# Linear attention into a gated FFN: first load in fp32 on another queue, narrow z matmuls, a new order on VectorE in the prologue, a new PSUM ring order, last stores on two queues

## Chip, cores, metric

One core of a Trainium2 chip. The metric is device time in microseconds (us), median of several runs. Engines: PE is TensorE (matmul; PEld its weight loads), DVE is VectorE, ACT is ScalarE, POOL is GpSimd, SP is SyncE, which issues DMAs.

## The reference

```python
def phi(x): return np.where(x > 0, x, np.exp(x) - 1.0) + 1.0
# q, k, v: [8 batches, 8 heads, 576 tokens, 64]
q_p, k_p = phi(q), phi(k)
kv  = einsum('bhsd,bhse->bhde', k_p, v)
z   = sum(k_p, axis=2)
num = einsum('bhsd,bhde->bhse', q_p, kv)
den = einsum('bhsd,bhd->bhs', q_p, z)[..., None] + 1e-06
x   = (num / den)  -> [4608 tokens, 512]
g   = x @ w_gate                                   # 512 -> 1536
out = (g / (1 + exp(-g)) * (x @ w_val)) @ w_out    # 1536 -> 512
```

## The kernel before

The tokens go through the FFN in nine groups of 512. While PE works on the FFN of one group, DVE and ACT prepare the next one. Group 0 has nothing to hide behind: its preparation is the *prologue*. Batches 0 and 1 get special code: phi(q) is transposed on PE, the reciprocal of den is exp(-ln(den)) on ACT.

The prologue (names: `mx_k`, `mn_k`, `add_k` are the DVE steps of phi(k); `zt` sums phi(k) over tokens by matmuls with a block of ones; `Zr` is z spread over 64 columns; `t_corners` multiplies with qT; `lnrd` is ln and exp on ACT; `warm` issues matmuls on ones whose results nothing uses):

```python
    WARM = (20, 8, 10, 2, 4)
    def warm(n):                        # n matmuls of 128x256 on ones
    def zt(b, lp, ps, t, first, last):
        for j in range(J):              # J = 9
            nc.tensor.matmul(out=ps[:, 0:P], lhsT=t[b % 2][:, lp, j, :], rhs=ob[:, :], ...)   # P = 128
    def lnrd(ps, i, w0=0, w1=512):
        for l2 in range(2):
            act(osb[2 * i + l2][:, w0:w1], ps[l2][:, w0:w1], AF.Ln, bias=epsb[:, 0:1])
            act(rd[i][:, l2, w0:w1], osb[2 * i + l2][:, w0:w1], AF.Exp, scale=-1.0)
    ...
    ld(q, qr, 0, 0)                     # POOL's queue, fp32 -> fp16 on the way
    ld(q, qr, 0, 1)
    ld2(k, kr, 0)
    ...
    mx_k(0, 0);  ph[1][1]();  zt(0, 0, .., kp, ..);  warm(WARM[3])
    t_add_half(1, pq[1], 0);  mn_k(0, 0);  zt(0, 0, .., ek, ..)
    add_k(0, 0);  zr_copy(0, 0, ..);  warm(WARM[4])
    t_add_half(1, pq[1], 1);  t_corners(0, Zr, 0, pp4[2]);  lnrd(pp4[2], 0)
    kv_corner(0, 0, ..);  mx_k(0, 1);  r_copy(0, 0, 1, "VV");  mn_k(0, 1);  t_corners(0, R, 0, pp4[0])
    ...
```

The seam between group 0 and group 1. PE holds four pairs of PSUM banks in a ring. `osb` are the tiles from which outputs are stored; before the change `lnrd` used them for its logarithms too:

```python
        def s7():
            ...
            exp_k(2, 0);  exp_k(2, 1)
            lnrd(cq, 0, 0, 256)                         # writes and reads osb[0], osb[1] on ACT
        def s8():
            for t in range(4):
                l2_out(0, t, "V")                       # DVE: PSUM -> osb[t], then stored
            xmul(xT[0] ..., cq ..., rd ...)             # two: the last two token blocks of group 1
        ...
        exp_q(2, 0);  exp_q(2, 1);  phi_k(2, 0);  phi_k(2, 1)
        ring[:] = [dz, cq, l2p[(0, "p", 0)], l2p[(0, "p", 1)]]
```

"Period 1" below is the FFN of group 1 and what runs beside it.

Of the kernel before, what the change touches and what calls it, by code (L numbers as in the profile page):

```python
# [13 lines left out]
P = 128  # L14
# [3 lines left out]
def kernel(  # L18
# [16 lines left out]
    C = 64  # L35
# [4 lines left out]
    EPS = 1e-6  # L40
    SC = 4096.0
    NB = 3
    WARM = (20, 8, 10, 2, 4)

    sb = ctx.enter_context(tc.tile_pool(name="sb", bufs=1))
    pp = ctx.enter_context(tc.tile_pool(name="ps", bufs=1, space=bass.MemoryType.PSUM))
# [15 lines left out]
    Zr = many([P, 2, 2, D], FP16, "Zr")  # L62
    rd = many([P, 2, 512], FP16, "rd")

    prod = sb.tile([P, J, 2 * D], FP16, name="prod")
    den = sb.tile([P, 2, J * 2], FP32, name="den")
    rden = sb.tile([P, 2, J * 2], FP32, name="rden")
# [30 lines left out]
    def ld(src, dst, b, lp):  # L98
        nc.gpsimd.dma_start(out=dst[b % NB][:, 2 * lp:2 * lp + 2, :],  # L99
                            in_=src[b].rearrange("(l a) (c j) d -> (a c) l (j d)", a=2, j=J)[:, 2 * lp:2 * lp + 2, :])  # L100
# [14 lines left out]
    def act(out, in_, func=AF.Copy, scale=1.0, bias=0.0):  # L115
        nc.scalar.activation(out=out, in_=in_, func=func, bias=bias, scale=scale)  # L116

    def warm(n):
        for _ in range(n):
            nc.tensor.matmul(out=pp4[2][1][:, :].rearrange("p (a b) -> p a b", a=4)[:, 0:2, :],  # L120
                             lhsT=ones[:, :], rhs=ones[:, :].unsqueeze(1).to_broadcast([P, 2, P]), start=True, stop=True)

    def hs(lp):
        return slice(2 * lp, 2 * lp + 2)
# [28 lines left out]
    def add_k(b, lp):  # L153
        a = kp[b % 2][:, lp, :, :]
        nc.vector.tensor_tensor(out=a, in0=ek[b % 2][:, lp, :, :], in1=a, op=ALU.add)  # L155
# [19 lines left out]
    def kv_corner(b, lp, t, first, last):  # L175
        ps = kvp[b]
        for j in range(J):
            for l2 in range(2):
                for hh in range(2):
                    rows = slice(C * hh, C * hh + C)  # L180
                    nc.tensor.matmul(out=ps[hh][D * l2:D * l2 + D, D * lp:D * lp + D],  # L181
                                     lhsT=t[b % 2][rows, lp, j, D * l2:D * l2 + D],
                                     rhs=vr[b % NB][rows, 2 * lp + l2, D * j:D * j + D],
                                     start=(first and j == 0), stop=(last and j == J - 1))
# [6 lines left out]
    def r_copy(b, l0, l1, engs):  # L191
        for hh in range(2):
            src = kvp[b][hh][:, D * l0:D * l1].rearrange("p (l d) -> p l d", d=D)
            if engs[hh] == "A":
                act(R[b % 3][:, l0:l1, hh, :], src)
            else:
                nc.vector.tensor_copy(out=R[b % 3][:, l0:l1, hh, :], in_=src)
# [112 lines left out]
    def l2_out(g, t, eng, n0=0, n1=512, o=None):  # L310
        if o is None:
            o = osb[on[0] % 4]
            on[0] += 1
        ps = l2p[(g, t)]
        if eng == "A":
            act(o[:, n0:n1], ps[:, n0:n1], scale=1.0 / SC)
        else:
            nc.vector.tensor_scalar(out=o[:, n0:n1], in0=ps[:, n0:n1], scalar1=1.0 / SC, scalar2=None, op0=ALU.mult)  # L318
        for e in range(2):
            b, j = units(g)[0][2 * t + e]  # L320
            nc.sync.dma_start(out=out[S * b:S * b + S, n0:n1].rearrange("(c j) f -> j c f", j=J)[j],
                              in_=o[C * e:C * e + C, n0:n1])
        return o



    ld(q, qr, 0, 0)
    ld(q, qr, 0, 1)
    nc.gpsimd.iota(out=idx[:, :], pattern=[[-1, P]], base=0, channel_multiplier=1)
    ld2(k, kr, 0)  # L330
# [49 lines left out]
    def t_phi_main(b, lp, ps):  # L380
        return t_phi(qT[b][:, lp, 0:8, :, :].rearrange("p j h c -> p (j h c)"), ps[:, :].bitcast(FP16))
# [4 lines left out]

    def zt(b, lp, ps, t, first, last):
        for j in range(J):
            nc.tensor.matmul(out=ps[:, 0:P], lhsT=t[b % 2][:, lp, j, :], rhs=ob[:, :],  # L389
                             start=(first and j == 0), stop=(last and j == J - 1))  # L390

    def zr_copy(b, lp, ps):
        nc.vector.tensor_scalar(out=Zr[b][:, lp, :, :].rearrange("p h e -> p (h e)"), in0=ps[:, 0:P],
                                scalar1=1.0 / SC, scalar2=None, op0=ALU.mult)

    def lnrd(ps, i, w0=0, w1=512):
        for l2 in range(2):
            act(osb[2 * i + l2][:, w0:w1], ps[l2][:, w0:w1], AF.Ln, bias=epsb[:, 0:1])
            act(rd[i][:, l2, w0:w1], osb[2 * i + l2][:, w0:w1], AF.Exp, scale=-1.0)

    def xmul(dst, ps, r):
        nc.vector.scalar_tensor_tensor(out=dst, in0=ps, scalar=1.0 / SC, in1=r, op0=ALU.mult, op1=ALU.mult)  # L402
# [5 lines left out]
    def t_corners(g, W, lp, ps):  # L408
        for (b, j0, j1, c0) in units(g)[1]:
            corners(ps, W[b], b, lp, j0, j1, c0)  # L410

    def t_add_half(lp, ps, h):
        a = qT[0][:, lp, 4 * h:4 * h + 4, :, :].rearrange("p j h c -> p (j h c)")
        nc.vector.scalar_tensor_tensor(out=a, in0=ps[:, 256 * h:256 * h + 256].bitcast(FP16), scalar=0.0, in1=a,  # L414
                                       op0=ALU.max, op1=ALU.add)

    pq = pp4[0]
    kvp[0] = pp4[1]
    ph = [t_phi_main(0, lp, pq[lp]) for lp in range(2)]
    warm(WARM[0])  # L420
    for lp in range(2):
        qtr(0, lp, pq[lp])
# [4 lines left out]
    ph[0][1]()  # L427
    ph[0][2]()
    mx_k(0, 0)
    ph[1][1]()  # L430
    zt(0, 0, pp4[3][0], kp, True, False)
    warm(WARM[3])
    t_add_half(1, pq[1], 0)
    mn_k(0, 0)
    zt(0, 0, pp4[3][0], ek, False, True)
    add_k(0, 0)
    zr_copy(0, 0, pp4[3][0])
    warm(WARM[4])
    t_add_half(1, pq[1], 1)
    t_corners(0, Zr, 0, pp4[2])  # L440
    lnrd(pp4[2], 0)
    kv_corner(0, 0, kp, True, True)
    mx_k(0, 1)
    r_copy(0, 0, 1, "VV")
    mn_k(0, 1)
    t_corners(0, R, 0, pp4[0])
    zt(0, 1, pp4[3][1], kp, True, False)
    zt(0, 1, pp4[3][1], ek, False, True)
    x_t(0, 0, pp4[0], (0,))
    zr_copy(0, 1, pp4[3][1])  # L450
    t_corners(0, Zr, 1, pp4[3])
    lnrd(pp4[3], 1)
    kv_corner(0, 1, kp, True, False)
# [28 lines left out]
    def p1_z():  # L482
        b1p["z"] = kvp[1] = pair()
        ring.pop()
        for lp in range(2):
            ps = b1p["z"][0]
            nc.tensor.matmul(out=ps[:, P * lp:P * lp + P], lhsT=zs[:, lp, 0, :], rhs=ob[:, :], start=True, stop=True)
        nc.vector.tensor_scalar(out=Zr[1][:, :, :, :].rearrange("p l h e -> p (l h e)"), in0=ps[:, 0:2 * P],
                                scalar1=1.0 / SC, scalar2=None, op0=ALU.mult)

    def period0():
# [28 lines left out]
    def layer2_0():  # L520
        for t in range(4):
            l2_open(0, t)
        p1_z()
        p1_open()
        cq, dz = b1p["q"], b1p["z"]
        p8 = [t_phi_8(b, dz[0]) for b in range(2)]
        pm = [t_phi_main(1, lp, cq[lp]) for lp in range(2)]
        nc.scalar.preload_act_table_set("natural_log_exp_and_others")

        def den(lp, ps):  # L530
            t_corners(1, Zr, lp, ps)
            lnrd(ps, lp)

        def kvr(lp):
            kv_corner(1, lp, kp, True, True)
            r_copy(1, lp, lp + 1, "VV")

        def nx(lp, ps):
            t_corners(1, R, lp, ps)
            x_t(1, lp, ps)  # L540

        def s0():
            qtr(1, 0, cq[0])
            for f in pm[0]:
                f()

        def s1():
            qtr8(dz[0])
            for f in (0, 1, 2):
                for b in range(2):  # L550
                    p8[b][f]()

        def s2():
            den(0, dz)

        def s3():
            qtr(1, 1, cq[1])
            for f in pm[1]:
                f()

        def s4():
            den(1, cq)

        def s5():
            kvr(0)

        def s6():
            kvr(1)
            nx(0, cq)

        def s7():
            nx(1, dz)
            for lp in range(2):
                corners(cq, Zr[1], 1, lp, 7, 9, P * lp)
                corners(cq, R[1], 1, lp, 7, 9, 256 + P * lp)
            exp_k(2, 0)
            exp_k(2, 1)
            lnrd(cq, 0, 0, 256)

        def s8():  # L580
            for t in range(4):
                l2_out(0, t, "V")
            for l2 in range(2):
                xmul(xT[0][:, l2::2, 0:P], cq[l2][:, 256:512].rearrange("p (l c) -> p l c", l=2),
                     rd[0][:, l2, 0:256].rearrange("p (l c) -> p l c", l=2))

        step = {1: [s0], 3: [s1, s3], 6: [s2], 7: [s4], 9: [s5], 10: [s6], 11: [s7]}
        for fb in range(FB):
            if fb in step:
                for f in step[fb]:  # L590
                    f()
            for t in range(4):
                l2_mm(0, t, fb)
        s8()
        exp_q(2, 0)
        exp_q(2, 1)
        phi_k(2, 0)
        phi_k(2, 1)
        ring[:] = [dz, cq, l2p[(0, "p", 0)], l2p[(0, "p", 1)]]

    for g in range(NG):
        b1, b2 = g + 1, g + 2
# [95 lines left out]
```

## Time and profile before

| | us |
|---|---|
| median time (3 runs) | 320.79 (320.46 to 321.27) |
| span in the profile | 319.0 |
| steady FFN matmuls begin (end of the prologue) | 22.02 |
| period 2 begins | 89.67 |
| last ACT copy ends / span ends | 315.37 / 319.0 |

From the page of the profile, part 1, the busy time of each engine and its share of the span; PE is the limit:

```profile
PE 307.7 (96%) x2240; PEld 145.9 (46%) x2240; DVE 203.5 (64%) x354; ACT 150.9 (47%) x227; POOL 49.2 (15%) x74
```

The list of PE's waits (who waited for whom: total, times, longest):

```profile
PE pp L364 <- DMA qr<-in_q_dram: 1.8, 2, 1.2
PE pp L288 <- DVE xT L402: 1.4, 1, 1.4
...
PE pp L181 <- issue: 0.8, 1, 0.8
```

Outside the prologue there is one wait of weight, 1.4 us for DVE's xT. The timeline around it (start, length, engine, line, operation, result<-operands, and in brackets the idle time before with what ended it):

```profile
53.44 1.04 PE L295 MATMUL pp<-wo,hT 128*128 128x512 f16 x4
53.60 0.45 ACT L116 ACTIVATE osb<-pp,epsb 128x256 f32<-128x256 f32 x1
54.09 0.42 ACT L116 ACTIVATE rd<-osb 128x256 f16<-128x256 f32 x1
...
54.32 1.03 PE L288 MATMUL pp<-xT,wg 128*128 128x512 f16 x4
...
54.54 2.70 DVE L318 TENSOR_SCALAR osb<-pp 128x512 f32<-128x512 f32 x4 [0.24 <-ACT rd L116]
...
57.15 0.75 DVE L402 SCALAR_TENSOR_TENSOR xT<-pp,rd 128x256 f16<-128x256 f32 x2
...
57.63 0.39 PE L288 MATMUL pp<-xT,wg 128*128 128x512 f16 x1 [1.42 <-DVE xT L402]
```

The second pair that PE asks for is `cq`, which the two xT operations at 57.15 still read.

The windows view (busy time of PE, PEld, DVE, ACT and POOL in a stretch, then granted clock, DMA share and GB/s) for 54.5 to 86 us:

```profile
54.50:86.00 31.50, 30.08 (x228) 13.70 (x229) 30.60 (x56) 18.60 (x28) 2.21 (x4) 1.00 0.58 117
```

DVE is busy 30.60 of 31.50 us here. It is the limit in this stretch as much as PE is.

The chain of waits that ended last has two marks of time (start, length, what): the first long run of FFN matmuls of group 0, and that of group 2.

```profile
22.02 17.27 PE pp L288 x80
...
89.67 20.72 PE pp L288 x96
```

### The profile page before, as it was taken

The numbers are of one execution on the slowest core, as the hardware profiler recorded it, in microseconds if no ns is written. First come the engines' busy times: TensorE is split into PE (matmuls) and PEld (weight loads), VectorE is DVE, ScalarE is ACT, GpSimd is POOL, SyncE is SP. The second block draws the span as 40 slices with busy tenths as digits, with TensorE's granted clock in tenths as the row PEclk, the third lists the DMA queues.
The fourth block names the chain that finished last, engine by engine and source line by source line (L and its number), as shares of the span: only waits on it lengthen the run. The fifth ranks groups of instructions, "written<-read, shape, count | busy, mean of one in ns | idle before, by whom it ended". The sixth has DMA issues, their size and how long they took to land.

```text
span 319.0 us, 5630 instructions
## 1 busy us (share of the span) xinstructions
PE 307.7 (96%) x2240; PEld 145.9 (46%) x2240; DVE 203.5 (64%) x354; ACT 150.9 (47%) x227; POOL 49.2 (15%) x74
## 2 busy tenths in 40 slices
PE   6789999899999999999999999999999999999994
PEld 4544444344544454444444454445444444444443
DVE  2844865999849874987498749973992344133410
ACT  2764859646643474347534753385331333133211
POOL 8665343000400050006000500000000000000000
PEclk9999999999999999999999999999999999999999
DMA  7999999931693379038903790225023400140014
GB/s 96 196 198 198 206 206 206 249 69 37 99 232 67 73 96 249 13 74 118 234 7 71 107 239 14 47 41 123 0 39 70 99 1 3 33 99 2 0 35 97
DMA packets 41162, 32.21 MB, mean 101 GB/s; under 512 B 16432, under 2 KB 36656, under 8 KB 41136
## 3 DMA queue, kind: packets, MB, share of 16 engines
q0 software_dynamic: 21008, 18.88, 38.6%
q1 hardware_dynamic: 20128, 12.98, 16.9%
q8 instruction: 17, 0.28, 0.3%
q14 instruction: 9, 0.07, 0.1%
HBM read 37.75 MB, written 9.44 MB: 148 GB/s over the span
## 4 chain that ended last, share of the span: by engine, by line
PE 93%; DVE 3%; DMA 2%; issue 1%; POOL 1%; ACT 0%; POOLq 0%; DVEq 0%
PE pp L288 57%; PE pp L295 29%; DMA kr<-in_k_dram 2%; PE pp L250 2%; PE pp L181 2%; PE pp L272 1%; DVE osb L318 1%; POOL qr L99 0%; DVE qT L414 0%; PE pp L389 0%; DVE xT L402 0%; PE pp L364 0%; DVE kp L139 0%; DVE kp L155 0%; PE pp L208 0%
## 5 line engine op out<-in xcount | busy, mean ns | idle before, releaser
L116 ACT ACTIVATE sil<-pp 128x512 f16<-128x512 f32 x108 | 63.4, 597 | 103.3 <-PE pp L288 98.8
L288 PE MATMUL pp<-xT,wg 128*128 128x512 f16 x424 | 108.8, 379 | 1.4 <-DVE xT L402 1.4
L288 PE MATMUL pp<-xT,wv 128*128 128x512 f16 x424 | 108.8, 379 | 0.0
L281 DVE SCALAR_TENSOR_TENSOR hT<-pp,sil 128x512 f16<-128x512 f32 x108 | 72.1, 681 | 47.8 <-PE pp L288 34.6
L295 PE MATMUL pp<-wo,hT 128*128 128x512 f16 (+1 forms) x444 | 97.5, 374 | 0.5 <-DVE osb L318 0.5
L288 PEld LDWEIGHTS <-wg 128*128 128x128 f16 x424 | 41.4, 98 | 51.1 <-DVE xT L402 1.9
L295 PEld LDWEIGHTS <-hT 128*128 128x128 f16 x444 | 42.1, 98 | 48.7 <-issue 1.9
L288 PEld LDWEIGHTS <-wv 128*128 128x128 f16 x424 | 41.5, 98 | 50.0
L318 DVE TENSOR_SCALAR osb<-pp 128x512 f32<-128x512 f32 (+1 forms) x20 | 13.3, 675 | 31.6 <-PE pp L295 26.8
L116 ACT ACTIVATE osb<-pp 128x512 f32<-128x512 f32 (+1 forms) x17 | 9.8, 578 | 34.9 <-PE pp L295 34.9
L116 ACT ACT_TABLE_LOAD x14 | 18.0, 1283 | 2.8 <-PE pp L288 2.6
L116 ACT ACTIVATE ek<-kr 128x1152 f16<-128x1152 f16 x16 | 17.8, 1154 | 0.3 <-DMA kr<-in_k_dram 0.2
L633 POOL COPY gate<-qT 128x1 f16<-128x1 f16 x4 | 1.3, 336 | 106.7 <-DMA qT<-qp 57.4
L225 DVE TENSOR_TENSOR qp<-qp,rden 128x1152 f16<-128x1152 f16 x12 | 16.2, 1346 | 0.0
L216 DVE TENSOR_REDUCE den<-prod 128x18 f32<-128x1152 f16 x12 | 16.1, 1345 | 0.0
L267 DVE TENSOR_SCALAR xT<-pp 128x512 f16<-128x512 f32 (+1 forms) x14 | 8.8, 667 | 7.3 <-PE pp L250 7.3
L116 ACT ACTIVATE eq<-qr 128x1152 f16<-128x1152 f16 x12 | 13.2, 1147 | 0.0
L99 POOL DMA_DIRECT2D kr<-in_k_dram x16 | 11.6, 726 | 6.8 <-DMA wo<-in_moe_w_out_dram 1.9
L99 POOL DMA_DIRECT2D vr<-in_v_dram x16 | 11.8, 742 | 5.2 <-DMA wo<-in_moe_w_out_dram 1.9
L99 POOL DMA_DIRECT2D qr<-in_q_dram x16 | 11.6, 729 | 6.0 <-DMA wo<-in_moe_w_out_dram 1.8
L155 DVE TENSOR_TENSOR kp<-ek,kp 128x1152 f16<-128x1152 f16 x15 | 11.4, 759 | 0.6
L143 DVE TENSOR_SCALAR ek<-ek 128x1152 f16<-128x1152 f16 x16 | 7.4, 463 | 4.8 <-ACT ek L116 4.8
(66 smaller groups left out, 175.6 us busy)
## 6 DMA issues: line engine op xcount, KB each, us to landing
out_dram<-osb SPq DMA_DIRECT2D x70, 128.0 KB, 5.3
qr<-in_q_dram POOLq DMA_DIRECT2D x16, 288.0 KB, 11.7
kr<-in_k_dram POOLq DMA_DIRECT2D x16, 288.0 KB, 6.6
vr<-in_v_dram POOLq DMA_DIRECT2D x16, 288.0 KB, 9.5
wo<-in_moe_w_out_dram POOLq DMA_DIRECT2D x3, 512.0 KB, 13.0
wg<-in_moe_w_gate_dram POOLq DMA_DIRECT2D x5, 256.0 KB, 9.6
wv<-in_moe_w_val_dram POOLq DMA_DIRECT2D x5, 256.0 KB, 10.2
wg<-in_moe_w_gate_dram POOLq DMA_DIRECT2D x2, 128.0 KB, 8.3
```

Of the source, the lines that this page charges most:

```text
L99: nc.gpsimd.dma_start(out=dst[b % NB][:, 2 * lp:2 * lp + 2, :], in_=src[b].rearrange("(l a) (c j) d -> (a c) l (j d)", a=2, j=J)[:, 2 * lp ...
L116: nc.scalar.activation(out=out, in_=in_, func=func, bias=bias, scale=scale)
L143: nc.vector.tensor_scalar(out=a, in0=a, scalar1=1.0, scalar2=None, op0=ALU.min)
L155: nc.vector.tensor_tensor(out=a, in0=ek[b % 2][:, lp, :, :], in1=a, op=ALU.add)
L181: nc.tensor.matmul(out=ps[hh][D * l2:D * l2 + D, D * lp:D * lp + D], lhsT=t[b % 2][rows, lp, j, D * l2:D * l2 + D], rhs=vr[b % NB][rows, 2 ...
L216: nc.vector.tensor_reduce(out=den[:, c, :], in_=prod[:, :, :].rearrange("p j (l d) -> p (j l) d", d=D), axis=AX.X, op=ALU.add)
L225: nc.vector.tensor_tensor(out=qv, in0=qv, in1=rden[:, c, :].unsqueeze(2).to_broadcast([P, 2 * J, D]), op=ALU.mult)
L267: nc.vector.tensor_scalar(out=dst, in0=ps[l2][:, c0:], scalar1=1.0 / SC, scalar2=None, op0=ALU.mult)
L281: nc.vector.scalar_tensor_tensor(out=hT[g % 2][:, fb, :], in0=ps[1][:, :], scalar=SC, in1=s[:, :], op0=ALU.mult, op1=ALU.mult)
L288: nc.tensor.matmul(out=ps[h][:, :], lhsT=w[:, c, P * fb:P * fb + P], rhs=xT[g % 2][:, c, :], start=(c == 0), stop=(c == 3))
L295: nc.tensor.matmul(out=l2p[(g, t)][:, n0:n1], lhsT=hT[g % 2][:, fb, P * t:P * t + P], rhs=wo[:, fb, n0:n1], start=(fb == 0), stop=(fb == F ...
L318: nc.vector.tensor_scalar(out=o[:, n0:n1], in0=ps[:, n0:n1], scalar1=1.0 / SC, scalar2=None, op0=ALU.mult)
```

## The change

Its intent: start the prologue earlier, get to the first Zr sooner, remove the wait for xT at 57 us, and issue the last two stores side by side. The diff, cut:

```diff
-    WARM = (20, 8, 10, 2, 4)
+    WARM = (36, 10, 20, 8, 6)
+    q32 = sb.tile([P, 2, J * D], FP32, name="q32")
+    lnt = many([P, 512], FP32, "lnt", 4)
     def warm(n):   # 128x256 -> 128x128 per matmul
-    ld(q, qr, 0, 0)
+    nc.sync.dma_start(out=q32[:, :, :], in_=q[0] ... [:, 0:2, :])
+    for l in range(2):
+        nc.vector.tensor_copy(out=qr[0][:, l, :], in_=q32[:, l, :])
     def zt(b, lp, ps, t, first, last):
-            nc.tensor.matmul(out=ps[:, 0:P], lhsT=t[b % 2][:, lp, j, :], rhs=ob[:, :],
+            nc.tensor.matmul(out=ps[:, 0:2], lhsT=t[b % 2][:, lp, j, :], rhs=ob[:, 0:P:C],
     def lnrd(ps, i, w0=0, w1=512):
-            act(osb[2 * i + l2][:, w0:w1], ps[l2][:, w0:w1], AF.Ln, bias=epsb[:, 0:1])
+            act(lnt[2 * i + l2][:, w0:w1], ps[l2][:, w0:w1], AF.Ln, bias=epsb[:, 0:1])
     ...  # batch 0 on DVE: mn_k before the min step of q's second half; zr_copy, then mx_k and mn_k of k's
     ...  # second half, before add_k(0, 0); the half adds of qT after that; z of batch 1 by 2 columns too
-        ring[:] = [dz, cq, l2p[(0, "p", 0)], l2p[(0, "p", 1)]]
+        ring[:] = [dz, l2p[(0, "p", 0)], l2p[(0, "p", 1)], cq]
-            nc.sync.dma_start(out=out[...], in_=o[...])
+            dma = nc.scalar if g == NG - 1 and t == 3 and n1 == 512 and e == 1 else nc.sync
+            dma.dma_start(out=out[...], in_=o[...])
```

More of the change, by code (lines that the diff above doesn't have):

```diff
@@ L119, in warm @@
         for _ in range(n):
-            nc.tensor.matmul(out=pp4[2][1][:, :].rearrange("p (a b) -> p a b", a=4)[:, 0:2, :],
-                             lhsT=ones[:, :], rhs=ones[:, :].unsqueeze(1).to_broadcast([P, 2, P]), start=True, stop=True)
+            nc.tensor.matmul(out=pp4[2][1][:, 0:P], lhsT=ones[:, :], rhs=ones[:, :], start=True, stop=True)
     def hs(lp):
@@ L320, in l2_out @@
             b, j = units(g)[0][2 * t + e]
-            nc.sync.dma_start(out=out[S * b:S * b + S, n0:n1].rearrange("(c j) f -> j c f", j=J)[j],
+            dma = nc.scalar if g == NG - 1 and t == 3 and n1 == 512 and e == 1 else nc.sync
+            dma.dma_start(out=out[S * b:S * b + S, n0:n1].rearrange("(c j) f -> j c f", j=J)[j],
                               in_=o[C * e:C * e + C, n0:n1])
         return o
-    ld(q, qr, 0, 0)
+    nc.sync.dma_start(out=q32[:, :, :],
+                      in_=q[0].rearrange("(l a) (c j) d -> (a c) l (j d)", a=2, j=J)[:, 0:2, :])
     ld(q, qr, 0, 1)
@@ L388, in zt @@
         for j in range(J):
-            nc.tensor.matmul(out=ps[:, 0:P], lhsT=t[b % 2][:, lp, j, :], rhs=ob[:, :],
+            nc.tensor.matmul(out=ps[:, 0:2], lhsT=t[b % 2][:, lp, j, :], rhs=ob[:, 0:P:C],
                              start=(first and j == 0), stop=(last and j == J - 1))
     def zr_copy(b, lp, ps):
-        nc.vector.tensor_scalar(out=Zr[b][:, lp, :, :].rearrange("p h e -> p (h e)"), in0=ps[:, 0:P],
+        nc.vector.tensor_scalar(out=Zr[b][:, lp, :, :], in0=ps[:, 0:2].unsqueeze(2).to_broadcast([P, 2, D]),
                                 scalar1=1.0 / SC, scalar2=None, op0=ALU.mult)
@@ L397, in lnrd @@
         for l2 in range(2):
-            act(osb[2 * i + l2][:, w0:w1], ps[l2][:, w0:w1], AF.Ln, bias=epsb[:, 0:1])
-            act(rd[i][:, l2, w0:w1], osb[2 * i + l2][:, w0:w1], AF.Exp, scale=-1.0)
+            act(lnt[2 * i + l2][:, w0:w1], ps[l2][:, w0:w1], AF.Ln, bias=epsb[:, 0:1])
+            act(rd[i][:, l2, w0:w1], lnt[2 * i + l2][:, w0:w1], AF.Exp, scale=-1.0)
     def xmul(dst, ps, r):
@@ L429 @@
     mx_k(0, 0)
-    ph[1][1]()
     zt(0, 0, pp4[3][0], kp, True, False)
     warm(WARM[3])
-    t_add_half(1, pq[1], 0)
     mn_k(0, 0)
     zt(0, 0, pp4[3][0], ek, False, True)
-    add_k(0, 0)
+    ph[1][1]()
     zr_copy(0, 0, pp4[3][0])
     warm(WARM[4])
-    t_add_half(1, pq[1], 1)
     t_corners(0, Zr, 0, pp4[2])
     lnrd(pp4[2], 0)
-    kv_corner(0, 0, kp, True, True)
     mx_k(0, 1)
-    r_copy(0, 0, 1, "VV")
     mn_k(0, 1)
-    t_corners(0, R, 0, pp4[0])
     zt(0, 1, pp4[3][1], kp, True, False)
     zt(0, 1, pp4[3][1], ek, False, True)
+    add_k(0, 0)
+    kv_corner(0, 0, kp, True, True)
+    zr_copy(0, 1, pp4[3][1])
+    t_add_half(1, pq[1], 0)
+    r_copy(0, 0, 1, "VV")
+    t_add_half(1, pq[1], 1)
+    t_corners(0, R, 0, pp4[0])
     x_t(0, 0, pp4[0], (0,))
-    zr_copy(0, 1, pp4[3][1])
     t_corners(0, Zr, 1, pp4[3])
@@ L486, in p1_z @@
             ps = b1p["z"][0]
-            nc.tensor.matmul(out=ps[:, P * lp:P * lp + P], lhsT=zs[:, lp, 0, :], rhs=ob[:, :], start=True, stop=True)
-        nc.vector.tensor_scalar(out=Zr[1][:, :, :, :].rearrange("p l h e -> p (l h e)"), in0=ps[:, 0:2 * P],
+            nc.tensor.matmul(out=ps[:, 2 * lp:2 * lp + 2], lhsT=zs[:, lp, 0, :], rhs=ob[:, 0:P:C],
+                             start=True, stop=True)
+        nc.vector.tensor_scalar(out=Zr[1][:, :, :, :].rearrange("p l h e -> p (l h) e"),
+                                in0=ps[:, 0:4].unsqueeze(2).to_broadcast([P, 4, D]),
                                 scalar1=1.0 / SC, scalar2=None, op0=ALU.mult)
```

## The prediction

> **What bounds the kernel.** TensorE: the busy table gives PE 96% of the 319.0 us span, and the chain that ended last is 93% PE (the two FFN matmul lines 57% and 29%). From 17.9 us PE hardly pauses, so a gain can come from three places only.
>
> 1. *Prologue.* The steady FFN matmuls begin at 22.0 us (timeline). The chain there: k's first half lands at 9.6, DVE work to 13.9, then Zr and R corners, ACT logarithms until 19.0, xT at 20.7. q's halves are first used at 5.3 and 8.1. From 3.5 us the DMA engines are full (190 GB/s written), with a dip to 95 GB/s from 6 to 8.
> 2. *The gap before period 1.* The list of PE's waits has 1.4 us, at 56.2 to 57.6, for DVE's xT: the second pair in the ring is the one DVE still reads.
> 3. *Tail.* The last ACT copy ends at 315.37; SP issues two stores one after the other (0.47 and 0.59 us), the second at 315.92, landing 2.0 later.
>
> **What the change does.**
>
> - *q in fp32 by SP's queue.* The bytes read from HBM stay. It frees one POOL issue of 0.78 us, so k, v and weights are issued that much earlier. [...]I expect no more bandwidth, only an earlier start. The price: two DVE casts, estimated at 0.4 to 0.6 us each from the 128x1152 fp16 operations (0.46 us; 0.58 beside POOL issues). First transposes at 5.5 to 6 us, second at 7, k at 8.7.
> - *DVE order, narrow z.* The first Zr comes before add_k (0.76 us) and a half add of qT (0.69), so the Zr corners start at about 11.5 instead of 12.7. [...]Prologue in all: 1.3 us (0.3 to 2.0).
> - *Ring order.* The 1.4 us wait goes. But the windows show DVE busy 30.6 of 31.5 us from 54.5 to 86.0, without a wait on PE over 0.25: the last hT of period 1 is ready at 78.96 by DVE's own work, and its matmul starts at 79.3 already. The second numerator pair at 85.7 needs DVE's copy that ends at 85.72. So nearly all of the 1.4 comes back as a wait of PE's layer-2 matmuls for hT near 78. Net 0.1 us (0 to 0.3).
> - *Last stores on two queues.* The second issue no longer follows the first: 0.5 us.
> - *Warm-up matmuls, separate lnt tiles:* nothing.
>
> **Sum.** 1.3 + 0.1 + 0.5 = 1.9 us: 318.9 us, 8 times in 10 within 317.6 to 320.1. Faster by over 2% (below 314.4) 2%, within 2% 97%, slower 1%.
>
> **What would show it.** PE's waits: none for xT at 56 us, but a new one of 1.2 to 1.5 us of the layer-2 line on DVE hT in period 1. Timeline: steady FFN matmuls from about 20.7 us; k at 8.5 to 9; Zr corners near 11.5. The span ends 0.5 us sooner after the last copy.
>
> **What would make it wrong.** The fp32 load shares engines with q's second quarter and lands after 6.5 us; [...]weights too late for the earlier start; a stall like the unexplained 0.8 us "issue" gap of PE at 16.9; or DVE slack in period 1 that I missed (then 1.3 us more).

To check two figures against the trace of before: from 3.5 to 6 us the core moved 191 GB/s at a DMA share of 1.18, and from 6.5 to 7.5 us, the dip, 94 to 97 GB/s. The "0.58 beside POOL issues" are the two DVE operations at 13.18 and 13.94 us, while POOL issued loads at 12.76, 13.49 and 14.22; what made them longer is not shown.

## The result

The changed kernel takes 319.39 us (318.84 to 319.74, 4 runs), before takes 320.62 us (320.26 to 321.27, 4 runs) in the same series: 1.2 us less. The ratio is 0.9958, 95% interval 0.9935 to 0.9980. Ratios here are the mean time of one kernel's runs over that of the other's of the same rounds, so not quite the ratio of the medians quoted.

PE's waits after:

```profile
PE pp L367 <- DMA qr<-in_q_dram: 1.3, 1, 1.3
...
PE pp L296 <- DVE hT L282: 0.3, 1, 0.3
...
PE pp L209 <- DVE zs L205: 0.3, 1, 0.3
```

The wait for xT is gone, and two new waits for DVE stand in its place. The timeline at the same seam and at the end of period 1:

```profile
53.89 2.47 DVE L319 TENSOR_SCALAR osb<-pp 128x512 f32<-128x512 f32 x4
...
55.73 1.03 PE L289 MATMUL pp<-xT,wg 128*128 128x512 f16 x4
...
56.29 0.74 DVE L405 SCALAR_TENSOR_TENSOR xT<-pp,rd 128x256 f16<-128x256 f32 x2
...
77.44 0.63 DVE L282 SCALAR_TENSOR_TENSOR hT<-pp,sil 128x512 f16<-128x512 f32 x1
...
78.12 2.98 PE L296 MATMUL pp<-wo,hT 128*128 128x512 f16 x13 [0.33 <-DVE hT L282]
```

PE starts its second pair at 55.73 instead of 57.63, 1.9 us sooner, but the last hT of the period comes at 77.44 + 0.63 and PE waits for it. The DVE copies start without a wait (no bracket) and take 2.47 instead of 2.70 us. The windows view, same stretch:

```profile
54.50:86.00 31.50, 30.92 (x285) 14.28 (x284) 30.77 (x57) 19.09 (x29) 3.15 (x5) 1.00 0.58 116
```

DVE is as full as before. The two marks of time:

```profile
21.76 17.27 PE pp L289 x80
...
88.81 20.72 PE pp L289 x96
```

So the 1.2 us between the spans (319.0 and 317.8) split into three terms: prologue 22.02 to 21.76 (-0.26); from there to period 2, 67.65 to 67.05 (-0.60); from period 2 to the end, 229.33 to 228.99 (-0.34). The prediction had -1.3, -0.1 and -0.5. The total fell in its range, but two of the three terms are wrong, in opposite directions.

One more thing shows in the windows by 1 us of the changed kernel. The third number from the end is the granted clock of PE:

```profile
core 0: us, PE busy (x) PEld busy (x) DVE busy (x) ACT busy (x) POOL busy (x), PEclk, DMA share, GB/s
...
14.00:15.00 1.00, 0.56 (x6) 0.24 (x8) 1.00 (x5) 0.91 (x2) 0.61 (x1) 1.00 1.44 194
15.00:16.00 1.00, 1.00 (x29) 0.72 (x32) 0.89 (x2) 0.34 (x1) 0.84 (x2) 0.51 1.45 196
16.00:17.00 1.00, 1.00 (x67) 0.94 (x59) 0.40 (x2) 0.97 (x3) 1.00 (x2) 0.50 1.46 197
17.00:18.00 1.00, 1.00 (x3) 0.33 (x3) 0.33 (x2) 0.97 (x3) 0.51 (x2) 0.50 1.44 195
18.00:19.00 1.00, 1.00 (x7) 0.17 (x6) 0.00 (x0) 0.98 (x2) 0.61 (x1) 0.78 1.49 210
```

From 15.0 to 18.4 us PE ran at half clock. Before the change the granted clock is 1.00 in all these windows. PE looks busier here (1.00 in each window from 15.0 us on), but each matmul takes longer: the first FFN matmuls of 512 columns take 0.61 to 0.63 us, 0.38 to 0.39 before. "Busy" is time, not work.

### The profile page after: what moved, and what is told of

It is laid out like the page before. It is cut to its first block, busy times and chain, and to the rows that moved or that the text cites. A ratio compares the mean times of both kernels' runs of the same rounds, so it can differ in the third digit from the quotient of the medians.

```text
span 317.8 us, 5702 instructions
## 1 busy us (share of the span) xinstructions
PE 309.0 (97%) x2276; PEld 147.4 (46%) x2276; DVE 203.5 (64%) x356; ACT 150.8 (47%) x227; POOL 48.7 (15%) x73
## 4 chain that ended last, share of the span: by engine, by line
PE 89%; DVE 6%; DMA 2%; ACT 1%; issue 1%; POOLq 0%
PE pp L289 54%; PE pp L296 29%; DMA qr<-in_q_dram 2%; PE pp L182 2%; PE pp L251 2%; PE pp L273 1%; DVE hT L282 1%; DVE osb L319 1%; DVE xT L405 1%; PE pp L367 1%; DVE kp L156 0%; DVE den L217 0%; DVE ek L144 0%; DVE qp L226 0%; DVE qT L417 0%
## 5 line engine op out<-in xcount | busy, mean ns | idle before, releaser
L101 POOL DMA_DIRECT2D kr<-in_k_dram x16 | 11.5, 722 | 6.3 <-DMA wo<-in_moe_w_out_dram 2.5
L101 POOL DMA_DIRECT2D qr<-in_q_dram x15 | 10.9, 729 | 5.9 <-DMA wo<-in_moe_w_out_dram 1.8
```

The lines of the kernel that those rows point to most:

```text
L101: nc.gpsimd.dma_start(out=dst[b % NB][:, 2 * lp:2 * lp + 2, :], in_=src[b].rearrange("(l a) (c j) d -> (a c) l (j d)", a=2, j=J)[:, 2 * lp ...
```

## The experiments

Theories. **A**: from 54.5 to 86 us DVE's own work sets the pace; what brings DVE's work forward counts, what lets PE run ahead does not. Then the 0.6 us came from the lnt tiles, not from the ring. **B** (rival): it came from the ring. **C**: with the narrow z PE's clock was halved, and this ate the prologue's gain. **D** (rival): the halved clock hides behind ACT and DVE.

All of them were timed against the kernel before, in series of five rounds, each series on one chip (four series, three chips); so a kernel is compared with another of a different series only by way of before. "T1" is the first mark of time (end of the prologue), "T1-T2" the stretch to period 2, "rest" from there to the end of the span, all from the profiled run. The last column is the range of the mean granted clock over all runs of the kernel.

| kernel | median us | ratio (95%) | T1 | T1-T2 | rest | clock |
|---|---|---|---|---|---|---|
| before | 320.5 to 320.8 | 1 | 22.02 | 67.65 | 229.33 | 0.993 to 1.0 |
| before + ring | 321.00 | 0.9996 (0.9967 to 1.0025) | 22.29 | 67.66 | 229.25 | 0.998 to 1.0 |
| before + lnt | 320.60 | 0.9980 (0.9947 to 1.0013) | 22.27 | 67.12 | 229.31 | 0.997 to 1.0 |
| before + ring + lnt | 320.24 | 0.9970 (0.9939 to 1.0000) | 21.24 | 67.12 | 229.34 | 0.998 to 1.0 |
| before + narrow z | 322.02 | 1.0041 (1.0020 to 1.0061) | 22.46 | 67.66 | 229.28 | 0.982 to 0.989 |
| changed | 319.80 | 0.9967 (0.9951 to 0.9982) | 22.23 | 67.08 | 229.09 | 0.987 to 0.995 |
| changed, one store queue | 319.65 | 0.9960 (0.9930 to 0.9990) | 22.16 | 67.06 | 229.28 | 0.987 to 0.995 |
| changed + fill | 320.51 | 0.9991 (0.9955 to 1.0026) | 21.74 | 67.04 | 228.92 | 0.984 to 0.998 |
| changed, wide z | 318.49 | 0.9929 (0.9916 to 0.9942) | 20.65 | 67.19 | 228.96 | 0.999 to 1.0 |
| changed, copies on ACT | 319.53 | 0.9955 (0.9941 to 0.9970) | 22.79 | 67.10 | 229.11 | 0.987 to 0.995 |
| changed, wide z, q by POOL | 318.69 | 0.9955 (0.9930 to 0.9980) | 20.52 | 67.03 | 229.05 | 0.995 to 1.0 |
| changed, wide z, old warm-ups | 319.17 | 0.9964 (0.9946 to 0.9982) | 20.73 | 67.07 | 229.00 | 0.992 to 1.0 |
| changed, wide z, max on ACT | 317.71 | 0.9905 (0.9890 to 0.9919) | 20.22 | 66.45 | 228.93 | 1.0 |

Read it by columns. T1-T2 and rest repeat within 0.2 us among kernels that share the code of that stretch, so differences of 0.5 us can be read from one profile. T1 does not: the prologues of before, of ring, of lnt and of both differ by nothing but the lnt tiles and end between 21.24 and 22.29. A single T1 is good to half a microsecond or so, which is why the runs' times and clocks have to carry the claims on the prologue.

### The ring alone

```diff
-        ring[:] = [dz, cq, l2p[(0, "p", 0)], l2p[(0, "p", 1)]]
+        ring[:] = [dz, l2p[(0, "p", 0)], l2p[(0, "p", 1)], cq]
```

> The kernel before with the new ring order alone. Theory A (DVE is full from 54.5 to 86 us, so the wait for xT only moves): the 1.4 us wait of PE at 56 us goes, waits for DVE's hT or zs of together about 1.2 us or more appear between 60 and 80 us, and period 2's first FFN matmul comes at most 0.3 us sooner than 89.67 us; time -0.0 to -0.3 us. Rival B (the ring order itself gave the 0.5 us that the changed kernel gained in period 1): period 2 starts 0.5 us or more sooner, time -0.5 us or more.

PE's waits from 50 to 90 us with the new ring alone; before there was one, the 1.4 us for xT:

```profile
PE pp L208 <- DVE zs L204: 0.8, 1, 0.8
PE pp L295 <- DVE hT L281: 0.3, 1, 0.3
```

The wait for xT became waits for zs and hT, 1.1 us in the list. T1-T2 is 67.66 against 67.65. The ring alone is worth nothing: a wait was moved, not removed. Rival B falls.

### The lnt tiles alone

```diff
-            act(osb[2 * i + l2][:, w0:w1], ps[l2][:, w0:w1], AF.Ln, bias=epsb[:, 0:1])
-            act(rd[i][:, l2, w0:w1], osb[2 * i + l2][:, w0:w1], AF.Exp, scale=-1.0)
+            act(lnt[2 * i + l2][:, w0:w1], ps[l2][:, w0:w1], AF.Ln, bias=epsb[:, 0:1])
+            act(rd[i][:, l2, w0:w1], lnt[2 * i + l2][:, w0:w1], AF.Exp, scale=-1.0)
```

> The kernel before with separate tiles for the logarithms alone, so that DVE's first output copy into osb no longer waits until ACT has read osb. Theory A: DVE's four output copies begin 0.25 us sooner after PE's last layer-2 matmul and run without gaps (2.47 instead of 2.70 us), xT of the last two units comes 0.4 to 0.6 us sooner, and with it PE's wait at 56 us shrinks from 1.4 to about 0.9 us; all DVE work of period 1 comes 0.4 to 0.6 us sooner; time -0.4 to -0.6 us. Rival B: nothing, under 0.2 us.

The timeline of this kernel at the seam:

```profile
53.69 1.04 PE L296 MATMUL pp<-wo,hT 128*128 128x512 f16 x4
...
54.45 2.48 DVE L319 TENSOR_SCALAR osb<-pp 128x512 f32<-128x512 f32 x4
...
56.85 0.75 DVE L403 SCALAR_TENSOR_TENSOR xT<-pp,rd 128x256 f16<-128x256 f32 x2
...
57.31 1.02 PE L289 MATMUL pp<-xT,wg 128*128 128x512 f16 x4 [0.86 <-DVE xT L403]
```

Its marks of time:

```profile
22.27 17.27 PE pp L289 x80
...
89.39 20.72 PE pp L289 x96
```

PE's last layer-2 group before the copies starts at 53.69 here and at 53.44 before. The copies start 0.76 us after it instead of 1.10, and take 2.48 instead of 2.70 us. T1-T2 falls by 0.53 us, from 67.65 to 67.12, within what theory A expected; PE's wait for xT is still there, 0.9 us long, and does not matter, as the next run shows. The timed ratio (0.9980) has the right size, but its interval includes 1; the stretch in the profile is what decides.

### Both

> Both alone, without the prologue and the tail of the change. Theory A: as lnt alone plus at most 0.3 us: -0.5 to -0.8 us, with no wait for xT and waits for DVE's hT and zs of about 0.9 us in its place. Rival B: -0.5 us, all of it already there with the ring alone.

T1-T2 is 67.12, the same as with the lnt tiles alone, and no shorter. The whole gain of period 1 is the lnt tiles'. Two tiles shared between ACT's scratch and DVE's outputs had held up DVE at the start of 24 us in which it had no slack. (Part of this run's lower time is its T1 of 21.24, which is scatter: its prologue has no part of the change but lnt, and k is first used at 9.07 us here, at 10.06 with lnt alone.)

### The last store on SP's queue again

```diff
-            dma = nc.scalar if g == NG - 1 and t == 3 and n1 == 512 and e == 1 else nc.sync
+            dma = nc.sync
```

> The changed kernel with its last store on SP's queue again. If the second queue saves the wait for the first issue, the span from the last ACT copy's end to the end grows from 3.29 back to 3.63 us, and the time is 0.3 to 0.4 us longer than the changed kernel's (319.4). If the second queue saves nothing (its own set-up eats it), the two spans are equal within 0.1 us.

From the end of the last ACT copy to the end of the span: before 319.0 - 315.37 = 3.63 us; this kernel 318.5 - 314.92 = 3.58; changed 317.8 - 314.51 = 3.29, and 318.4 - 315.14 = 3.26 in its repeat. The second queue is worth 0.3 us. The column "rest" agrees: 228.92 to 229.11 us in the eight profiles with the second queue, 229.25 to 229.34 in the six without. The timed medians (319.65 here, 319.80 for the repeat of the changed kernel on another chip) can't show that: the scatter of the clock in the prologue, next, is larger.

### The changed kernel again, with fill, and with wide z

> The changed kernel again, as the control of this series: 319.4 us, -1.2 us against before, granted clock 0.5 for 3.4 us somewhere between 14 and 19 us.

The repeat gave 319.80 us. All of its six runs have a mean clock of 0.987 to 0.995. In the profiled one the clock was halved from 13.1 to 19.9 us, twice as long as in the first profile.

Fill, nine more matmuls on ones in two gaps of PE, into unused columns of a bank:

```diff
+    def fill(n):
+        for _ in range(n):
+            nc.tensor.matmul(out=kvp[0][1][:, 256:384], lhsT=ones[:, :], rhs=ones[:, :], start=True, stop=True)
     kv_corner(0, 0, kp, True, True)
+    fill(5)
     ...
     t_corners(0, R, 0, pp4[0])
+    fill(4)
```

> The changed kernel with nine more warm-up matmuls in two idle gaps of PE (13.8 to 14.2 and 14.7 to 15.0 us), into unused columns of a bank. Theory C ([...]the clock was halved for 3.4 us, and that took back some 1.2 us of the prologue's gain): the granted clock stays 1.0 from 14 to 19 us, the steady FFN matmuls begin near 20.4 instead of 21.6 us, time -1.0 to -1.3 us against the changed kernel. [...]the clock halves as before and nothing changes. Rival D (the halved clock is hidden behind ACT's logarithms and DVE): clock 1.0, but the FFN matmuls begin within 0.3 us of 21.6.

"The clock halves as before" is the other outcome, a fill without effect.

The clock was halved in this kernel too (from 14.5 to 17.9 us in the profile), and the times scatter more than any other's, 318.02 to 321.98 us. The run with the highest mean clock, 0.998, was the fastest and the one with the lowest, 0.984, the slowest. As a remedy it failed; it says nothing for D.

Wide z, only the narrow matmuls of batch 0 undone:

```diff
-            nc.tensor.matmul(out=ps[:, 0:2], lhsT=t[b % 2][:, lp, j, :], rhs=ob[:, 0:P:C],
+            nc.tensor.matmul(out=ps[:, 0:P], lhsT=t[b % 2][:, lp, j, :], rhs=ob[:, :],
-        nc.vector.tensor_scalar(out=Zr[b][:, lp, :, :], in0=ps[:, 0:2].unsqueeze(2).to_broadcast([P, 2, D]),
+        nc.vector.tensor_scalar(out=Zr[b][:, lp, :, :].rearrange("p h e -> p (h e)"), in0=ps[:, 0:P],
```

> The changed kernel with z of batch 0 by 128 columns again. Theory C with the narrow z as its cause: [...]the clock stays at 1.0 until 19 us, and the time falls by 0.7 to 1.2 us although z takes 0.3 us longer twice. If narrow z is not the cause, the clock is halved as before and the time grows by 0 to 0.4 us.

The first z matmuls of the changed kernel and of the one with wide z, and the first Zr corners of each (PE view of the timeline):

```profile
9.76 0.39 PE L392 MATMUL pp<-ob,kp 128*128 128x2 f16 x9
...
11.91 0.41 PE L251 MATMUL pp<-qT,Zr 64*64 64x512 f16 x4
```

```profile
9.90 0.68 PE L392 MATMUL pp<-ob,kp 128*128 128x128 f16 x9 [0.40 <-DVE kp L140]
...
12.00 0.41 PE L251 MATMUL pp<-qT,Zr 64*64 64x512 f16 x4
```

The windows by 1 us of the kernel with wide z:

```profile
14.00:15.00 1.00, 0.34 (x2) 0.21 (x3) 1.00 (x4) 0.97 (x2) 0.51 (x1) 1.00 1.44 195
15.00:16.00 1.00, 0.80 (x34) 0.52 (x34) 1.00 (x3) 0.16 (x2) 0.95 (x2) 1.00 1.42 192
16.00:17.00 1.00, 1.00 (x69) 0.72 (x57) 0.93 (x3) 0.97 (x2) 1.00 (x2) 1.00 1.46 197
17.00:18.00 1.00, 1.00 (x8) 0.30 (x7) 0.02 (x1) 0.97 (x3) 0.50 (x2) 1.00 1.44 195
18.00:19.00 1.00, 1.00 (x6) 0.41 (x5) 0.98 (x2) 0.98 (x2) 0.51 (x1) 1.00 1.45 196
```

The clock stays at 1.00, with 0.999 to 1.0 in all five runs. The median is 318.49 us, 1.3 us below the changed kernel in the same series, and the times lie within 0.8 us. Theory C expected 0.7 to 1.2 us. T1 is 20.65, 1.4 us sooner than before: that is the size that I had predicted for the prologue. A steadier mark than T1 is the stretch from the first Zr corners to T1, because the scatter of the loads lies before it. It takes 8.65 us with wide z (8.65 and 8.66 with q by POOL and with max on ACT), but 9.85 in the changed kernel and 10.21 to 10.98 in its repeat and its three other variants with narrow z. D falls: what the clock costs is not hidden.

### Narrow z alone, on the kernel before

The same edit the other way round, in the kernel before, with all else as it was.

> The kernel before with the narrow z of batch 0 alone, all else as it was. Theory C: taking 36 wide matmuls out of the prologue is enough for the clock to halve: granted clock 0.5 for 3.4 us or more between 13 and 19 us in most runs (mean clock 0.995 or lower), time +0.5 to +1.5 us. Rival: [...]clock as before (0.997 to 1.0), time within 0.3 us.

The rival is that the new DVE order, not the narrow z, halves the clock.

Two of its windows; before, the first of them has a clock of 1.00:

```profile
14.00:15.00 1.00, 1.00 (x21) 0.56 (x21) 0.58 (x2) 0.99 (x2) 0.63 (x1) 0.50 1.39 194
...
18.00:19.00 1.00, 1.00 (x4) 0.30 (x2) 0.20 (x2) 0.95 (x3) 0.71 (x2) 0.50 1.44 196
```

The clock was half from about 12.2 to 19.0 us. All six runs have a mean of 0.982 to 0.989, where before has 0.997 to 1.0 in the same series, and the time grew by 0.41%, 1.2 us by the medians. From the first Zr corners to T1 it takes 10.07 us, against 9.10 to 9.37 in the kernel before and its three other variants. So the narrow z is enough to halve the clock without the new order, and taking it out of the changed kernel kept it whole in all five runs. It is not the only thing that can lower it. Counted over every run with narrow z, 33 of 34 have a mean clock of 0.995 or less; without it 4 of 83 have: one of the 44 runs of before in these series (0.993, 323.72 us) and three of the two variants of wide z at the end of this section.

In the windows by 1 us of these profiles the granted clock is 0.50 or 1.00, apart from the windows in which it changes. It is low for 3.4 us in the changed kernel (15.0 to 18.4) and with fill (14.5 to 17.9), and for 6.8 us with narrow z alone (12.2 to 19.0) and in the repeat (13.1 to 19.9). What sets it is not shown. The longest wait of PE before the clock fell was 1.3 us in the changed kernel. PE's busy time, as the profile counts it, does not sort the cases: in the 3.4 us before the clock fell PE was busy 1.73 us with narrow z alone, 2.45 in the changed kernel and 3.03 with fill, and 2.65 (11.6 to 15.0 us) with wide z, where it did not fall. Replacing 128 columns by 2 takes nearly all of the columns away and leaves over half of the time: 9 wide z matmuls took 0.68 us, 9 narrow ones 0.39, of which their weight loads are busy 0.30.

### Two of DVE's output copies on ACT

```diff
-                l2_out(0, t, "V")
+                l2_out(0, t, "VVAA"[t])
```

> The changed kernel with two of DVE's four output copies before period 1 done by ACT. Theory A (DVE's backlog sets the end of period 1): DVE's work from there on comes 1.2 to 1.3 us sooner, PE's waits for zs and hT in period 1 go, time -0.5 to -1.0 us against the changed kernel. Rival: ACT, which has the exponentials and a table load there, becomes the limit instead and the first silu comes 1.2 us later: 0 or worse.

No gain: T1-T2 is 67.10. The rival was right. The timeline of this kernel shows DVE held up by ACT's first silu instead:

```profile
59.15 1.28 ACT L118 ACT_TABLE_LOAD   x1
...
60.44 2.06 ACT L118 ACTIVATE sil<-pp 128x512 f16<-128x512 f32 x4
...
61.07 1.29 DVE L282 SCALAR_TENSOR_TENSOR hT<-pp,sil 128x512 f16<-128x512 f32 x2 [1.13 <-ACT sil L118]
```

In the first 5.5 us of the stretch (54.5 to 60) ACT is as full as DVE: 5.44 and 5.43 us busy in the changed kernel. So work may only be given to it later.

### The maxima of q on ACT, in ACT's slack

On top of wide z. After the first silus ACT waits 1.13 us for PE in each block, while DVE is full:

```diff
+    def phi_q_a(b, lp):
+        a = qr[b % NB][:, hs(lp), :]
+        act(a, a, AF.Relu)
+        mn_q(b, lp)
+        add_q(b, lp)
-                sl[4] = [lam(phi_q, b1, 0), lam(zb, b1)]
-                sl[5] = [lam(phi_q, b1, 1)]
+                sl[4] = [lam(phi_q_a, b1, 0)]
+                sl[5] = [lam(phi_q_a, b1, 1), lam(zb, b1)]
```

> The changed kernel with wide z, and in period 1 the two maxima of q with zero (2 x 0.45 us) moved from DVE to ACT where ACT waits for PE, and the matmul that sums z one slot later. Theory A (DVE's backlog sets the end of period 1, ACT only in its first 5 us): PE's waits for zs (0.3) and hT (0.3 in the list, with the records missing more) go or shrink, from the first steady FFN matmul to period 2's takes 66.2 to 66.6 instead of 67.1 us, time -0.5 to -0.9 us against the wide kernel, 317.6 to 318.0. Rival: another limit stands right behind (the transposed qT, ACT): 0 to -0.2 us.

The marks of time and the stretch:

```profile
20.22 17.27 PE pp L295 x80
...
86.67 20.72 PE pp L295 x96
```

```profile
54.50:86.00 31.50, 31.33 (x288) 14.59 (x287) 28.50 (x52) 19.94 (x31) 4.70 (x7) 1.00 0.63 124
```

The same stretch with wide z alone:

```profile
54.50:86.00 31.50, 30.90 (x284) 14.27 (x283) 29.80 (x55) 18.57 (x29) 4.12 (x7) 1.00 0.61 120
```

T1-T2 is 66.45, 0.74 us less than with wide z alone (and 0.58 less than the lowest of the others), and PE is busy 31.33 of 31.50 us there, DVE 28.50. The time is 317.71 us (317.38 to 318.00), ratio 0.9905 to before: 3.1 us less than before by the medians of that series, and the best kernel. (Wide z alone was timed in another series; the two intervals just overlap, so the step between them is read from T1-T2.) It agrees with A: DVE had been the limit. The edit also moves the z matmul one slot later, which alone was not run; but from its first output copy to its last hT DVE now needs 22.96 us instead of 23.56, and moving a matmul on PE takes no work off DVE. One maximum takes 1.156 us on ACT and 0.45 us on DVE, so per operation DVE is the faster engine; here it paid to give the two maxima to the engine that had the slack. They brought no table load: 16 in this kernel and in the one with wide z.

### q by POOL again, and the old warm-ups, both with wide z

The first undoes the fp32 load and its casts:

```diff
-    nc.sync.dma_start(out=q32[:, :, :], in_=q[0] ... [:, 0:2, :])
+    ld(q, qr, 0, 0)
-    for l in range(2):
-        nc.vector.tensor_copy(out=qr[0][:, l, :], in_=q32[:, l, :])
```

> The changed kernel with wide z (318.5 us in the series before, clock 1.0), and q's first quarter again as POOL's first load in fp16, without the two casts. If the fp32 load on SP's queue is worth what the earlier issue of k is worth, k lands 0.3 to 0.4 us later and the steady FFN matmuls begin 0.3 to 0.5 us later than the 20.65 us of the wide kernel: time +0.3 to +0.5 us. Rival: the load and its casts cancel (casts of 1.1 us, second quarter held back by the fp32 load): within 0.2 us.

T1 is 20.52 against 20.65. The median is 318.69 against 318.49 in another series; two of the six runs have a lowered clock (0.995) and 319.9 and 320.9 us, the other four lie between 318.3 and 318.9. In the runs with the full clock no loss is visible, as the rival said; but k is first used at 9.10 us here and at 9.39 with wide z, the loads scatter by more than that, and 0.3 us either way is not excluded. Whether the fp32 load and its casts do anything for the clock is not shown.

The second puts back the counts and the width of the warm-ups of before:

```diff
-    WARM = (36, 10, 20, 8, 6)
+    WARM = (20, 8, 10, 2, 4)     # and 256 columns each in place of 128
```

> The changed kernel with wide z and with the warm-up matmuls of before (20, 8, 10, 2, 4 of 256 columns in place of 36, 10, 20, 8, 6 of 128). If the new DVE order alone gives the prologue's 1.4 us and the warm-ups nothing, as the prediction had it, the clock stays at 1.0, the steady FFN matmuls begin within 0.3 us of 20.65 us and the time is within 0.3 us of the wide kernel's 318.5. [...]the clock halves between 12 and 19 us in some or all runs, and the time is 0.5 to 1.5 us longer.

The last sentence is the other outcome, in which the old warm-ups cost time.

Inconclusive. The profiled run has the clock at 1.00 from 10 to 20 us and T1 at 20.73, within 0.1 us of the new warm-ups, but needs 9.13 us from the first Zr corners to T1, where they need 8.65. One run of six fell to 0.992 (320.77 us). But the other five, with 0.998 to 1.0, took 318.6 to 319.3 us, where wide z took 318.0 to 318.9 on another chip. Whether the new warm-ups are worth some 0.4 us without any halved clock is open.

## Why the prediction was right, and where it was not

The total, 318.9 us with 317.6 to 320.1, held: 319.39 was measured. Its terms did not hold as well:

- **Prologue, "1.3 us (0.3 to 2.0)": measured 0.26 in the profile, below the stated range.** The mechanism was right in part: the first Zr corners came at 11.9 us (11.5 predicted, 12.7 before), and with wide z the prologue ends 1.4 us sooner. The step that failed is the price of narrow z: an estimate of mine of 0.5 us for 9 matmuls, after the 0.50 to 0.51 us that the weight loads of 9 wide ones take before, and no other effect. Its size is off (9 narrow ones take 0.39 us against 0.68 for wide ones, and their weight loads 0.30 against 0.51), and it is beside the point: with narrow z PE's clock was half for 3.4 to 6.8 us in the profiles, which cost 1.3 us (wide against narrow z in the changed kernel). I priced the operation by its duration only, and did not ask what else would change with it.
- **What of the prologue's gain is the fp32 load's:** first transposes were predicted at 5.5 to 6 us and came at 4.93 (5.29 before), the second at 7.83 (7 predicted; 8.14 before), k at 9.24 (8.7 predicted; 9.64 before). From 3 to 4 us the fp32 load moved 0.26 MB with 68.9% of the 16 engines' time and POOL's queue 0.02 MB with 26.8% (before, POOL's queue alone moved 0.14 MB in that microsecond, with 96.2%; in all 278 GB/s against 143), but in the end the loads' scatter is larger than any effect: the second transposes begin at 7.08 to 8.08 us in the eight profiles with the fp32 load and at 7.03 to 8.65 in the six without, and k is first used at 8.97 to 9.49 and at 9.07 to 10.06. Undone, it made no visible difference in runs with the full clock. Of the 1.4 us with wide z, k's arrival is 0.25; from k to the first Zr corners it takes 2.61 us instead of 3.08, and from there to T1 8.65 instead of 9.30. These two stretches are where the new order on DVE acts, but it was never run alone, and the part of the new warm-ups in it is open.
- **Ring, "Net 0.1 us (0 to 0.3)": right, 0.0 measured,** and for the stated reason. The wait "of 1.2 to 1.5 us of the layer-2 line on DVE hT" was misplaced in part: it is shared between zs at 63 us and hT at 78, of which the list shows 0.3 each in the changed kernel, 0.8 and 0.3 with the ring alone.
- **Separate lnt tiles, "nothing": wrong, 0.53 us.** The line "0.24 <-ACT rd" stood at the head of DVE's full stretch. In the same paragraph I had argued that DVE's backlog sets the end of period 1; by that very argument each wait of DVE at its start counts in full.
- **Tail, "0.5 us": measured 0.3 us.** The second issue no longer waits 0.52 us for the first (315.40 and 315.92 before), but the store on ACT's queue took 2.2 us from issue to landing, against 2.0 for the second store on SP's queue before, so not all of it is won.

That the total fell in its range is in part luck: the prologue brought 1.0 us less than forecast and the tail 0.2 less, period 1 brought 0.5 us more, by tiles that the prediction gave nothing, and the range was 2.5 us wide.

## What to carry to other kernels

Where two engines are both nearly full, as here, removing a wait of one may only move it: find the engine whose own work sets the end of the stretch, and look at the first microsecond of its run for small waits such as a scratch tile shared with another engine. When matmuls are made smaller or removed, as z's were here, look at the granted clock of every run before looking at durations: the mean clock of the whole run (0.982 to 0.995 in 33 of the 34 runs with narrow z, 0.997 to 1.0 in 43 of the 44 runs of before) is enough to see it. And a sum that comes out right can hide terms that are wrong in both directions, so check each term against its own mark in the profile.
